# Sparse attention followed by a three-way max layer: bf16 value copies on VectorE and another order of the units

## The chip, the cores and the metric

The kernel runs on one core of a Trainium2 chip. The time is the device time of one execution in microseconds (us); of several executions the median is given. A profile of one execution comes beside it: its span is the time from the first to the last instruction of the program.

## What is computed

Attention over 4 batches, 8 heads, 768 positions of 64 numbers each. A position sees the first 8 positions of its batch (global) and the last 96 up to itself (local); each head subtracts its own slope times the distance. The rows of the result, 3072 of 512 numbers, go through a layer that takes the largest of three products and then multiplies by an output matrix.

```python
scores = scale * np.matmul(q, k.transpose(0, 1, 3, 2))
keep = is_global | is_local
scores = np.where(keep, scores + bias, -1000000000.0)
a = softmax(scores)
x = np.matmul(a, v).transpose(0, 2, 1, 3).reshape(3072, 512)
h = np.maximum(np.maximum(x @ w1, x @ w2), x @ w3)    # 512 -> 768
out = h @ w_out                                       # 768 -> 512
```

## The kernel before, in words

The 3072 rows are cut into 24 tiles T of 128 rows, six to a batch. Attention for a tile needs its own keys and those of the tile in front of it, with four global rows copied over four old ones. Two tiles share one load n (n = T/2). The feed-forward layer works on seven chunks of 4, 2, 2, 4, 4, 4 and 4 tiles, so its matmuls have 512 or 256 moving columns.

The whole program is a list of about 500 small units, the string `SCHEDULE` (lines 25 to 60). A loop at line 538 calls them in the order of the list. Every engine takes its own instructions strictly in that order, so the list sets all queues at once: TensorE (PE), VectorE (DVE), ScalarE (ACT), GpSimd (POOL) and SyncE (SP), which issues nearly all DMAs. The last number of a unit mostly names its engine: 0 is ScalarE, 1 is VectorE, 2 is GpSimd. The letters:

- `l`, `v`, `w`, `o` load queries and keys, values, the three weight matrices and the output matrix (SP, lines 155 to 174 and 477 to 488). `c`, `C`, `W`, `Q` cast what they brought to bf16 (lines 178 to 190, 490 to 495).
- `x` transposes queries or keys of one load (line 242): with a last number of 6, 7 or 8 by sixteen matmuls on half the rows and two copies, one per half of the rows (6: ScalarE and VectorE; 7: both ScalarE; 8: both VectorE); with 2 or 3 by eight full matmuls and one copy on ScalarE or VectorE; with 9 by a DMA transpose on SP.
- `S` computes the scores of four heads of a tile and their exponentials (ScalarE, line 316). With a last number of 1 the distances are added on TensorE from `bias` (made by `B`, line 318); otherwise `M` (line 328) multiplies by `wmask` (made by `K`, line 323) on VectorE.
- `Y` copies rows of values into the layout that even tiles need (line 198), `G` and `V` put the global keys and values in place (lines 228 and 234), `Z` copies the first keys of a batch (line 206).
- `A` multiplies by the values (line 359) and divides by the sum (VectorE, lines 371 and 372). `T` transposes the result into `xT` (line 375): with 0 or 1 on TensorE and one copy, with 6 to 8 in half rows, with 4 by a DMA transpose on SP (line 380).
- `F` is one of 126 blocks of the first layer (line 416): four matmuls into a buffer `psH`, of which there are three; the first of three products is copied by ScalarE (428), the other two are folded in by VectorE (430, 432). `O` is one tile of the output (450) and its store on SP; `E` is the last chunk's outputs (455).
- `D` with a count makes so many matmuls of 512 columns on constants (line 501), whose result nobody reads.

`F3.1.2` is then chunk 3, block 1 of 6, product 2; `S16.1.0` is tile 16, group 1, without the bias; `T22.4` is the DMA transpose of tile 22.

The copies of the values (`Y`, `V`) go through `same` (line 192): on VectorE and GpSimd two bf16 numbers are moved as one int32 word, on ScalarE as bf16.

Of the kernel before, what the change touches and what calls it, by code (L numbers as in the profile page):

```python
# [22 lines left out]


SCHEDULE = """
    K4 B3.1 K3 c0.0.2 B0.1 B4.1 K6 B6.2 K1 K0 K7 B1.0 B2.1 K2 B7.0 D7.3 D3.3 D0.8 c0.1.1 K5 x0.1.8
    B5.0 l1.1 c1.1.0 D8.2 x0.0.6 D4.2 S1.0.1 l1.0 c1.0.1 M1.0 Z0.1 S1.1.1 M1.1 x1.1.3 v0 C0.0.1 G1.0
    C0.1.1 x1.0.6 S0.0.1 M0.0 S2.1.1 v1 C1.0.1 Y0.1.2 Y0.0.2 Y1.0.1 V2.2 S2.0.1 G2.0 C1.1.2 A1.2
    Y1.1.2 l2.1 S0.1.1 S3.0.1 M3.0 c2.1.2 V3.2 M2.0 M0.1 A0.2 S3.1.1 G3.0 M3.1 M2.1 A2.0 l2.0 x2.1.7
    c2.0.2 w0.0 T0.1 W0.0.2 w0.1 A3.1 T2.0 x2.0.6 T1.0 T3.1 S4.1.0 Y2.0.1 S4.0.0 G4.1 F0.1.0 F0.0.0  # L30
    S5.1.0 W0.1.1 w0.2 S5.0.0 M4.1 F0.0.1 w1.0 W2.0.0 W1.0.0 M5.1 v2 F0.1.1 W0.2.2 C2.1.0 F0.0.2
    C2.0.0 F0.1.2 M5.0 Y2.1.1 F0.5.0 M4.0 V5.0 w1.1 F0.4.0 F0.3.0 V4.1 W1.1.1 F0.2.0 W2.1.0 A5.1
    A4.0 F0.3.1 F0.2.1 w1.2 W2.2.1 l3.1 F0.5.1 W1.2.0 T5.0 F0.4.1 c3.1.0 T4.0 F0.5.2 x3.1.2 l3.0
    c3.0.1 F0.3.2 l4.1 c4.1.1 F1.2.0 F1.2.1 Z1.0 x3.0.7 l4.0 c4.0.1 F0.4.2 F1.4.0 S7.1.0 x4.0.6
    S7.0.0 F1.4.1 F1.2.2 v3 C3.1.1 F1.1.0 l5.0 c5.0.1 G7.1 F1.1.1 S6.1.0 M6.1 Y3.1.1 x4.1.7 S6.0.0
    F0.2.2 F1.0.0 M7.0 x5.0.7 S8.1.0 M7.1 S8.0.0 G8.0 F1.1.2 F1.4.2 C3.0.2 F1.0.1 F1.5.0 Y3.0.1 o2
    l5.1 c5.1.1 A7.1 F1.3.0 F1.3.1 o0 Q0.1 F1.5.1 o1 Q1.1 Q2.0 M6.0 x5.1.7 S9.1.0 v4 S9.0.0 G9.0
    C4.1.0 M8.1 F1.0.2 T7.1 C4.0.0 F1.3.2 l6.1 v5 l7.0 l6.0 l7.1 l8.0 O0.2.0 A6.1 Y4.0.1 V8.1 O0.3.0
    c6.1.1 x6.1.9 M9.0 M8.0 O0.0.0 T6.6 v6 S10.1.0 S10.0.0 G10.1 Y5.0.1 Y4.1.1 F1.5.2 M10.1 V9.1
    O0.1.0 c7.0.1 M10.0 A8.1 T8.4 F2.1.0 F2.5.0 C5.0.1 x7.0.9 F2.4.0 F2.0.0 c6.0.0 F2.0.1 F2.4.1  # L40
    F2.5.1 M9.1 S11.1.0 c7.1.0 S11.0.0 x6.0.6 F2.1.1 F2.5.2 C5.1.1 A9.1 T9.4 F2.3.0 Y5.1.1 M11.0
    M11.1 O1.0.0 F2.3.1 F2.3.2 S13.0.0 S13.1.0 C6.0.0 x7.1.6 V10.1 v7 v9 F2.0.2 V11.1 Z2.0 F2.1.2
    F2.2.0 G13.1 A10.0 A11.1 O1.1.1 T10.6 S12.0.0 S12.1.0 M13.0 F2.4.2 F2.2.1 C6.1.1 c8.0.1 v8 l9.0
    Y7.0.1 T11.7 l8.1 l9.1 S14.0.0 S14.1.0 F2.2.2 F3.0.0 F3.4.0 M12.0 F3.2.0 C7.0.0 G14.0 Y6.1.0
    M13.1 A13.0 M14.0 C7.1.0 V14.1 F3.4.1 M14.1 F3.0.1 F3.0.2 T13.4 S15.1.0 S15.0.0 O2.0.0 l10.1
    Y7.1.1 V15.1 F3.1.0 C8.0.0 M15.0 M15.1 F3.2.1 C8.1.0 Y8.1.0 A14.0 A15.1 T15.4 Y6.0.1 M12.1
    O2.1.1 C9.1.0 F3.2.2 c8.1.1 F3.5.0 F3.3.0 A12.0 Y9.1.1 F3.3.1 F3.3.2 c9.1.0 c9.0.0 F3.4.2 F3.1.1
    F3.5.1 C9.0.0 F3.5.2 F3.1.2 T14.4 T12.4 F4.0.0 x9.1.9 Z3.1 G15.1 F4.4.0 F4.4.1 x9.0.9 F4.4.2
    S19.1.0 S19.0.0 F4.0.1 M19.1 Y10.0.1 M19.0 F4.2.0 F4.2.1 S18.0.0 S18.1.0 F4.0.2 x8.1.9 x8.0.9
    S16.0.0 M18.1 S16.1.0 G16.1 F4.1.0 l10.0 V17.1 c10.0.1 c10.1.1 Y9.0.0 M16.0 l11.0 F4.5.0 F4.3.0  # L50
    l11.1 c11.1.1 v10 x10.0.9 x10.1.9 A19.1 O3.1.0 v11 F4.5.1 x11.1.9 T19.4 c11.0.1 x11.0.9 M18.0
    S17.1.0 S17.0.0 M17.1 O3.2.0 M17.0 V20.1 Y8.0.0 F4.3.1 F4.3.2 V16.0 G19.0 A18.1 T18.4 F4.1.1
    A17.0 C10.0.0 O3.3.0 M16.1 C11.1.1 F4.2.2 C10.1.0 S20.0.0 T17.4 S20.1.0 G20.0 Y10.1.1 F4.1.2
    F4.5.2 A16.2 Y11.0.0 M20.1 C11.0.0 S21.1.0 S21.0.0 G21.1 T16.4 O3.0.0 V22.1 M21.0 O4.1.0 M21.1
    M20.0 O4.0.1 Y11.1.1 S22.1.0 S22.0.0 G22.1 F5.5.0 V21.1 F5.0.0 O4.2.0 F5.0.1 M22.1 V23.0 O4.3.0
    A20.2 T20.4 M22.0 S23.0.0 M23.0 S23.1.0 M23.1 F5.3.0 F5.4.0 A21.0 T21.4 F5.0.2 F5.3.1 F5.3.2
    F5.2.0 F5.2.1 A22.1 A23.0 T23.4 T22.4 F5.2.2 F5.5.1 F5.1.0 F5.1.1 F5.1.2 F5.5.2 F5.4.1 F5.4.2
    F6.0.0 F6.4.0 O5.2.0 F6.1.0 F6.3.0 F6.3.1 F6.1.1 F6.3.2 F6.5.0 O5.1.0 F6.5.1 F6.5.2 F6.0.1
    F6.0.2 F6.2.0 F6.2.1 F6.4.1 F6.4.2 O5.3.1 F6.1.2 F6.2.2 O5.0.0 E D9.1
"""  # L60


# [1 line left out]
def kernel(  # L64
# [13 lines left out]
    nc = tc.nc  # L78
# [63 lines left out]
    def words(ap):  # L142
        return ap.bitcast(mybir.dt.int32)
# [32 lines left out]
    copies = (nc.scalar.copy, nc.vector.tensor_copy, nc.gpsimd.tensor_copy)  # L176
# [13 lines left out]
        copies[how](heads(vo(n)[:, e * H * 65:(e + 1) * H * 65])[:, :, 0:D], rawv[n][:, :, e * D:(e + 1) * D])  # L190

    def same(how, dst, src):
        if how:
            copies[how](words(dst), words(src))  # L194
        else:
            nc.scalar.copy(dst, src)

    def u_Y(n, half, how):
        b, k = divmod(n, 3)
        rows = slice(64 * half, 64 * half + 64)  # L200
        if k == 0:
            same(how, vf[b % 2][rows], vo(n)[0:64, half * H * 65:(half + 1) * H * 65])
        else:
            same(how, ve[k - 1][rows], vo(n - 1 + half)[64 - 64 * half:128 - 64 * half])
# [29 lines left out]
    def put_vg(T, how):  # L234
        n, hi = divmod(T, 2)
        dst = (vo(n) if hi else ve[n % 3 - 1])[0:NG // 2]
        same(how, dst, vo(n - n % 3)[0:NG // 2])
# [335 lines left out]
```

## Time and profile before

| | us |
|---|---|
| median of 3 runs | 175.34 (175.29 to 175.38) |
| the profiled execution, its own time | 175.3 |
| span of that execution | 173.5 |
| TensorE busy in the span | 168.0 |
| VectorE busy | 130.2 |
| ScalarE busy | 119.6 |
| GpSimd busy | 12.4 |

The profiled execution's time is 1.8 us above its span, and within 0.04 us of the median. The profile counts an engine as busy while an instruction of its own runs; matmuls overlap, so the distance between the starts of two matmuls tells what one costs, not its duration. In a line of a timeline the first number is the start, the second the length of the merged stretch, and brackets hold the idle time before it and who ended it. L423 is line 423 of the kernel.

### The profile page before, as it was taken

To read this page: it belongs to the slowest core of one execution; us is meant where nothing else is said; L and a number is where in the kernel's file an instruction comes from. 1 tells how busy PE (TensorE), PEld (TensorE's weight loads), DVE (VectorE), ACT (ScalarE), POOL (GpSimd) and SP (SyncE) were. 2 spreads that over 40 slices of the span, in tenths; PEclk is the share of its full clock that TensorE was granted. 3 is DMA by queue.
4 is the path that set the end of the run, shared out by engine and by line. 5 is a ranking of instruction groups with operands and counts; after the bars stand their busy time and mean duration, and the time that the engine had idled before them with its cause. 6 is when DMAs were issued, how large, how long until landed. Compare 5 with 4: busy or idle time off the path is not lost.

```text
span 173.5 us, 4167 instructions
## 1 busy us (share of the span) xinstructions
PE 168.0 (97%) x1636; PEld 93.0 (54%) x1659; DVE 130.2 (75%) x285; ACT 119.6 (69%) x192; POOL 12.4 (7%) x23
## 2 busy tenths in 40 slices
PE   8999999999999999999999999999999999999992
PEld 3345744567775777654544445455455544444442
DVE  6477859998999999979998496997759773346600
ACT  6998999889998898797780576978975112321042
POOL 5417520001000000000000000000000000000000
PEclk9999999999999999999999999999999999999999
DMA  4999999999999996979969899995423120110126
GB/s 122 343 299 339 360 349 384 387 343 389 313 289 292 255 247 167 285 198 293 204 163 170 202 292 186 214 198 132 160 92 95 32 60 0 60 60 0 64 80 222
DMA packets 56595, 36.18 MB, mean 209 GB/s; under 512 B 19456, under 2 KB 49024, under 8 KB 56576
## 3 DMA queue, kind: packets, MB, share of 16 engines
q1 hardware_dynamic: 55392, 35.33, 77.1%
q10 hardware_dynamic: 1184, 0.59, 1.3%
q8 instruction: 13, 0.21, 0.5%
q14 instruction: 6, 0.05, 0.1%
HBM read 25.17 MB, written 6.29 MB: 181 GB/s over the span
## 4 chain that ended last, share of the span: by engine, by line
PE 77%; DVE 12%; ACT 7%; issue 2%; POOL 0%; POOLq 0%; ACTq 0%; DVEq 0%
PE h L423 50%; PE po L438 14%; PE sp L305 5%; PE op L359 4%; ACT P L316 3%; DVE P L333 3%; ACT wmask L325 2%; DVE h L430 1%; DVE ve L194 1%; DVE xb L372 1%; PE tpr L260 1%; DVE qkp L187 1%; PE xtp L410 1%; DVE ht L432 1%; ACT bias L321 1%
## 5 line engine op out<-in xcount | busy, mean ns | idle before, releaser
L423 PE MATMUL h<-xT,w 128*128 128x512 bf16 (+1 forms) x491 | 99.6, 348 | 0.9 <-DVE h L430 0.2
L423 PEld LDWEIGHTS <-w 128*128 128x128 bf16 x504 | 47.1, 98 | 42.1 <-issue 0.4
L316 ACT ACTIVATE P<-sp 128x1024 bf16<-128x1024 f32 (+1 forms) x48 | 44.1, 964 | 6.2 <-PE sp L305 5.9
L428 ACT CAST h<-h 128x512 bf16<-128x512 f32 (+1 forms) x42 | 21.6, 537 | 26.5 <-PE h L423 26.0
L430 DVE TENSOR_TENSOR h<-h,h 128x512 bf16<-128x512 bf16 (+1 forms) x42 | 25.2, 606 | 19.5 <-PE h L423 16.8
L438 PE MATMUL po<-wo,ht 128*128 128x512 bf16 (+2 forms) x147 | 33.1, 362 | 0.5
L432 DVE TENSOR_TENSOR ht<-h,h 128x512 bf16<-128x512 bf16 (+1 forms) x42 | 25.3, 607 | 3.1 <-PE h L423 2.0
L333 DVE TENSOR_TENSOR P<-P,wmask 128x1024 bf16<-128x1024 bf16 x34 | 22.6, 682 | 1.6 <-ACT P L316 1.5
L438 PEld LDWEIGHTS <-ht 128*128 128x128 bf16 x156 | 14.3, 98 | 14.4
L447 ACT COPY ost<-po 128x512 f32<-128x512 f32 (+2 forms) x21 | 11.7, 566 | 13.9 <-PE po L438 13.4
L359 PEld LDWEIGHTS <-P 128*128 128x128 bf16 x352 | 12.9, 97 | 3.8 <-ACT P L316 0.4
L372 DVE TENSOR_TENSOR xb<-op,rz 128x512 bf16<-128x512 f32 x20 | 13.8, 691 | 0.7
L305 PE MATMUL sp<-qkT 64*128 64x128 bf16 x320 | 13.1, 217 | 0.0
L305 PEld LDWEIGHTS <-qkT 64*128 64x128 bf16 x320 | 9.2, 94 | 6.4 <-issue 4.0
L187 DVE CAST qkp<-rawp 128x1024 bf16<-128x1024 f32 x15 | 10.2, 681 | 2.1 <-DMA rawp<-in_k_dram 1.3
L503 PE MATMUL wp<-const-bfloat16-1.0 128*128 128x512 bf16 x18 | 7.5, 574 | 0.8 <-PEq L554 0.8
L447 DVE COPY ost<-po 128x512 f32<-128x512 f32 (+1 forms) x5 | 3.0, 607 | 6.1 <-PE po L438 6.1
L267 ACT COPY qkT<-tpr 128x512 bf16<-128x512 bf16 x12 | 6.8, 616 | 0.0
L190 ACT CAST vo<-rawv 128x512 bf16<-128x512 f32 x11 | 6.6, 638 | 0.0
L187 ACT CAST qkp<-rawp 128x1024 bf16<-128x1024 f32 x6 | 6.2, 1042 | 0.0
L371 DVE RECIPROCAL rz<-op 128x8 f32<-128x8 f32 x20 | 4.0, 198 | 1.7 <-PE op L359 1.7
L359 PE MATMUL op<-vo,P 128*128 128x65 bf16 x128 | 5.2, 193 | 0.0
(86 smaller groups left out, 118.9 us busy)
## 6 DMA issues: line engine op xcount, KB each, us to landing
rawv<-in_v_dram SPq DMA_DIRECT2D x12, 512.0 KB, 7.0
out_dram<-ost SPq DMA_DIRECT2D x23, 256.0 KB, 2.5
rawp<-in_k_dram SPq DMA_DIRECT2D x8, 512.0 KB, 7.6
rawp<-in_q_dram SPq DMA_DIRECT2D x12, 256.0 KB, 6.4
wst<-in_moe_w_dram SPq DMA_DIRECT2D x3, 1024.0 KB, 11.5
rawp<-in_q_dram SPq DMA_DIRECT2D x6, 512.0 KB, 6.8
wst<-in_moe_w_dram SPq DMA_DIRECT2D x3, 512.0 KB, 8.4
rawp<-in_k_dram SPq DMA_DIRECT2D x6, 256.0 KB, 8.6
```

The costliest lines, as they stand in the source:

```text
L187: copies[how](qk, src)
L305: nc.tensor.matmul(sp[:, z, i, ds], k_cols(T, hsl, jp, ds), q_cols(T, hsl, jp), start=not how, stop=True, skip_group_check=True)
L316: nc.scalar.activation(dst, src, AF.Exp, bias=0.0, scale=scale)
L333: nc.vector.tensor_mul(P, P, wmask[:, g, :, 0:2])
L359: nc.tensor.matmul(o, P[:, i, ds], vs[ds][:, h], start=(ds == 0), stop=(ds == len(vs) - 1), skip_group_check=True)
L372: nc.vector.tensor_tensor(out=x.rearrange("p (g h) d -> p g h d", g=2), in0=o4[:, :, :, 0:64], in1=rz[:, :, :, None].to_broadcast([128, 2, ...
L423: nc.tensor.matmul(ps, w123[f // 2][:, dm, j, (f % 2) * 128:(f % 2) * 128 + 128], xT[c][:, dm], start=(dm == order[0]), stop=(dm == order[ ...
L428: nc.scalar.copy(h01, ps)
L430: nc.vector.tensor_max(h01s[c, f], h01s[c, f], ps)
L432: nc.vector.tensor_max(ht[c][:, f], h01s[c, f], ps)
L438: nc.tensor.matmul(po, ht[c][:, f, tt * 128:(tt + 1) * 128], wo[:, f, cols], start=(f == 0), stop=(f == NF - 1))
L447: copy(ost, po)
```

## The change

`same` now moves values on VectorE as bf16, twice as many elements of half the size; GpSimd still moves int32 words, ScalarE bf16. The list of units is put into another order, and 71 units get another engine or form. No unit is added or dropped, save that the idle matmuls of `D` are split otherwise.

```diff
     def same(how, dst, src):
-        if how:
-            copies[how](words(dst), words(src))
-        else:
-            nc.scalar.copy(dst, src)
+        if how == 2:
+            nc.gpsimd.tensor_copy(words(dst), words(src))
+        else:
+            copies[how](dst, src)
```

The beginning of the list, before and after (up to the first `F`):

```diff
-    K4 B3.1 K3 c0.0.2 B0.1 B4.1 K6 B6.2 K1 K0 K7 B1.0 B2.1 K2 B7.0 D7.3 D3.3 D0.8 c0.1.1 K5 x0.1.8
-    B5.0 l1.1 c1.1.0 D8.2 x0.0.6 D4.2 S1.0.1 l1.0 c1.0.1 M1.0 Z0.1 S1.1.1 M1.1 x1.1.3 v0 C0.0.1 G1.0
-    C0.1.1 x1.0.6 S0.0.1 M0.0 S2.1.1 v1 C1.0.1 Y0.1.2 Y0.0.2 Y1.0.1 V2.2 S2.0.1 G2.0 C1.1.2 A1.2
-    Y1.1.2 l2.1 S0.1.1 S3.0.1 M3.0 c2.1.2 V3.2 M2.0 M0.1 A0.2 S3.1.1 G3.0 M3.1 M2.1 A2.0 l2.0 x2.1.7
-    c2.0.2 w0.0 T0.1 W0.0.2 w0.1 A3.1 T2.0 x2.0.6 T1.0 T3.1 S4.1.0 Y2.0.1 S4.0.0 G4.1 F0.1.0 F0.0.0
+    l1.1 D0.8 B0.0 K4 K5 B5.2 K2 B7.1 D6.4 D7.1 D1.2 K0 B2.1 c0.1.1 K6 c0.0.1 K3 K1 B4.1 B6.0 B1.1
+    K7 B3.1 x0.1.2 x0.0.6 D8.2 S1.0.1 M1.0 S1.1.1 l1.0 M1.1 c1.0.1 G1.0 c1.1.2 Z0.1 x1.1.3 x1.0.6
+    S0.0.1 S2.1.1 S2.0.1 v0 C0.1.2 Y0.1.1 G2.0 C0.0.1 Y0.0.1 Y1.0.1 M0.0 A1.2 D5.1 S0.1.1 S3.0.1
+    M0.1 A0.2 v1 S3.1.1 C1.1.2 M2.0 M3.1 M2.1 C1.0.2 Y1.1.2 V2.2 A2.0 l2.1 c2.1.2 x2.1.7 V3.2 l2.0
+    c2.0.2 w0.0 W0.0.2 G3.0 T0.1 M3.0 A3.1 w0.1 w0.2 W0.1.2 T1.0 x2.0.7 T2.1 T3.1 S4.0.0 M4.0
+    S4.1.0 G4.0 F0.0.0 Y2.0.1 F0.1.0 F0.0.1 F0.1.1 V4.0 w1.0 W1.0.1 F0.0.2 M4.1 v2 C2.0.1 F0.1.2
```

Of the rest, these places are spoken of below (new list, TensorE's and SP's units and what feeds them):

```diff
+    x3.1.2 F0.4.2 Z1.0 l4.0 c4.0.0 x3.0.6 F0.5.2 T4.4 F1.4.0 l4.1 F1.2.0 S7.1.0 c4.1.1 S7.0.0 x4.0.6
...
+    Y8.0.0 F3.4.2 O2.0.0 O2.1.0 M15.1 M15.0 A12.1 G15.1 V16.1 C8.0.0 T12.4 M14.0 c9.0.1 F3.2.0
+    F3.0.0 c8.1.0 V14.1 F3.5.2 x8.1.9 F3.3.0 A15.1 F3.3.1 T15.4 A14.0 F3.0.1 F3.0.2 c9.1.0 C9.0.0
+    T14.4 x9.0.9 F3.2.1 F3.1.2 F3.2.2 c8.0.0 C9.1.0 C8.1.0 F4.4.0 F4.5.0 F4.4.1 F3.3.2 x9.1.9
+    S19.1.0 S19.0.0 M19.1 F4.2.0 F4.5.1 x8.0.9 S16.1.0 S16.0.0 G16.1 l10.1 v11 v10 M16.0 Z3.1 l10.0
...
+    M23.0 O4.2.0 F5.5.1 F5.5.2 A23.0 F5.4.0 V22.1 F5.0.1 A22.1 T23.4 F5.2.2 F5.0.2 F5.3.2 F5.4.1
+    F5.4.2 T22.4 F6.0.0 F6.0.1 F6.5.0 F6.5.1 F6.4.0 F6.3.0 F6.0.2 F6.1.0 F6.1.1 O5.3.0 O5.2.0 F6.3.1
...
+    F6.3.2 F6.4.1 F6.5.2 F6.1.2 F6.4.2 F6.2.0 O5.0.0 F6.2.1 F6.2.2 O5.1.1 E D2.6
```

The old list had `T4.0` in the place of `T4.4`, and ended in `F6.1.2 F6.2.2 O5.0.0 E D9.1`.

More of the change, by code (lines that the diff above doesn't have):

```diff
@@ L31 @@
[L31 to L59, printed above, removed]
+    l1.1 D0.8 B0.0 K4 K5 B5.2 K2 B7.1 D6.4 D7.1 D1.2 K0 B2.1 c0.1.1 K6 c0.0.1 K3 K1 B4.1 B6.0 B1.1
@@ new lines @@
+    K7 B3.1 x0.1.2 x0.0.6 D8.2 S1.0.1 M1.0 S1.1.1 l1.0 M1.1 c1.0.1 G1.0 c1.1.2 Z0.1 x1.1.3 x1.0.6
+    S0.0.1 S2.1.1 S2.0.1 v0 C0.1.2 Y0.1.1 G2.0 C0.0.1 Y0.0.1 Y1.0.1 M0.0 A1.2 D5.1 S0.1.1 S3.0.1
+    M0.1 A0.2 v1 S3.1.1 C1.1.2 M2.0 M3.1 M2.1 C1.0.2 Y1.1.2 V2.2 A2.0 l2.1 c2.1.2 x2.1.7 V3.2 l2.0
+    c2.0.2 w0.0 W0.0.2 G3.0 T0.1 M3.0 A3.1 w0.1 w0.2 W0.1.2 T1.0 x2.0.7 T2.1 W0.2.2 T3.1 S4.0.0 M4.0
+    S4.1.0 G4.0 F0.0.0 Y2.0.1 F0.1.0 F0.0.1 F0.1.1 V4.0 w1.0 W1.0.1 F0.0.2 M4.1 v2 C2.0.1 F0.1.2
+    W2.0.0 S5.1.0 M5.1 S5.0.0 M5.0 F0.4.0 C2.1.0 Y2.1.1 V5.1 F0.5.0 w1.1 F0.3.0 W2.1.1 F0.2.0 A4.1
@@ new lines @@
+    A5.0 F0.5.1 W1.1.0 w1.2 W1.2.0 F0.4.1 W2.2.1 F0.3.1 F0.2.1 F0.3.2 l3.1 c3.1.0 T5.0 l3.0 c3.0.1
+    x3.1.2 F0.4.2 Z1.0 l4.0 c4.0.0 x3.0.6 F0.5.2 T4.4 F1.4.0 l4.1 F1.2.0 S7.1.0 c4.1.1 S7.0.0 x4.0.6
+    F1.2.1 F1.4.1 F1.2.2 G7.0 F1.0.0 M7.1 F1.1.0 l5.0 c5.0.1 S6.1.0 x4.1.6 S6.0.0 v3 C3.0.2 M7.0
+    F1.0.1 F0.2.2 x5.0.7 C3.1.1 S8.1.0 S8.0.0 G8.0 F1.1.1 F1.1.2 o0 l5.1 o2 Y3.0.1 F1.4.2 c5.1.1
+    F1.0.2 F1.5.0 A7.1 Q2.0 o1 v4 v5 F1.3.0 F1.5.1 x5.1.7 Q0.1 Q1.1 S9.0.0 Y3.1.0 C4.0.0 S9.1.0
+    F1.5.2 M6.0 M6.1 F1.3.1 F1.3.2 G9.1 l6.1 T7.0 l7.0 l6.0 l7.1 O0.1.0 M8.0 C4.1.0 A6.0 M9.0 M9.1
@@ new lines @@
+    O0.0.0 Y4.1.1 c6.1.1 S10.0.0 T6.8 S10.1.0 x6.1.9 O0.2.0 M8.1 M10.0 v6 V9.1 O0.3.0 F2.4.0 F2.3.0
+    Y4.0.0 M10.1 F2.4.1 C5.0.1 G10.0 F2.4.2 V8.1 c6.0.0 A9.1 T9.4 F2.0.0 F2.0.1 c7.0.1 F2.5.0
+    S11.0.0 x6.0.6 S11.1.0 F2.3.1 Y5.0.1 V10.1 F2.0.2 F2.1.0 A8.0 M11.1 T8.4 C5.1.0 Y5.1.1 c7.1.0
+    O1.1.0 V11.1 M11.0 x7.0.9 v7 l8.0 F2.2.0 F2.1.1 S13.1.0 S13.0.0 x7.1.6 Z2.0 G13.1 F2.1.2 F2.2.1
+    A10.1 A11.2 C6.1.1 O1.0.0 S12.0.0 T10.8 v8 S12.1.0 F2.5.1 C6.0.1 F2.5.2 F2.3.2 l8.1 l9.1 l9.0
+    T11.6 v9 S14.0.0 S14.1.0 M13.1 M13.0 F2.2.2 Y6.1.1 M12.1 C7.0.1 F3.5.0 Y6.0.1 C7.1.0 F3.4.0
@@ new lines @@
+    A13.0 T13.4 F3.1.0 G14.1 F3.5.1 M14.1 S15.1.0 Y7.1.1 V15.0 S15.0.0 F3.4.1 M12.0 Y7.0.0 F3.1.1
+    Y8.0.0 F3.4.2 O2.0.0 O2.1.0 M15.1 M15.0 A12.1 G15.1 V16.1 C8.0.0 T12.4 M14.0 c9.0.1 F3.2.0
+    F3.0.0 c8.1.0 V14.1 F3.5.2 x8.1.9 F3.3.0 A15.1 F3.3.1 T15.4 A14.0 F3.0.1 F3.0.2 c9.1.0 C9.0.0
+    T14.4 x9.0.9 F3.2.1 F3.1.2 F3.2.2 c8.0.0 C9.1.0 C8.1.0 F4.4.0 F4.5.0 F4.4.1 F3.3.2 x9.1.9
+    S19.1.0 S19.0.0 M19.1 F4.2.0 F4.5.1 x8.0.9 S16.1.0 S16.0.0 G16.1 l10.1 v11 v10 M16.0 Z3.1 l10.0
+    F4.1.0 Y8.1.0 M19.0 O3.3.1 F4.1.1 c10.1.1 l11.1 S18.1.0 M18.1 S18.0.0 F4.1.2 l11.0 F4.4.2 Y9.0.1
@@ new lines @@
+    Y9.1.0 C10.1.0 A19.1 T19.4 F4.3.0 F4.3.1 O3.0.0 x10.1.9 M18.0 G19.0 M16.1 S17.1.0 c10.0.0
+    x10.0.9 S17.0.0 M17.1 F4.2.1 F4.2.2 M17.0 C10.0.1 F4.0.0 F4.0.1 A18.1 T18.4 V17.0 Y10.1.1 F4.5.2
+    c11.1.0 Y10.0.0 F4.3.2 O3.1.0 A17.1 C11.0.1 V20.1 x11.1.9 C11.1.0 O3.2.0 c11.0.1 x11.0.9 T17.4
+    F4.0.2 S20.0.0 S20.1.0 G20.1 A16.2 Y11.1.1 Y11.0.0 T16.4 O4.0.1 S21.0.0 M21.0 S21.1.0 G21.1
+    O4.3.1 O4.1.0 M20.1 M21.1 M20.0 S22.0.0 M22.0 S22.1.0 F5.1.0 F5.0.0 V21.1 M22.1 G22.1 F5.5.0
+    F5.2.0 A20.0 V23.0 F5.1.1 F5.1.2 A21.0 F5.2.1 T21.4 F5.3.0 F5.3.1 T20.4 S23.1.0 M23.1 S23.0.0
```

## The prediction

> **What bounds the kernel now.** First the page's head and the engines by stretch, then the chain that ended last, then single rows of the timelines.
>
> ```profile
> span 173.5 us, 4167 instructions
> ...
> PE 168.0 (97%) x1636; PEld 93.0 (54%) x1659; DVE 130.2 (75%) x285; ACT 119.6 (69%) x192; POOL 12.4 (7%) x23
> ...
> PE 77%; DVE 12%; ACT 7%; issue 2%; POOL 0%; POOLq 0%; ACTq 0%; DVEq 0%
> ```
>
> The engines by stretch (start:end, length, then busy us of each):
>
> ```profile
> 8.00:20.85 12.85, 12.50 (x229) 7.55 (x223) 9.72 (x26) 12.23 (x22) 7.15 (x10) 1.00 1.13 332
> 20.85:47.00 26.15, 25.89 (x282) 15.65 (x288) 22.53 (x45) 24.39 (x39) 1.71 (x2) 1.00 1.08 364
> 47.00:67.00 20.00, 19.84 (x282) 14.34 (x284) 19.70 (x47) 17.89 (x32) 0.00 (x0) 1.00 1.21 264
> 67.00:98.00 31.00, 30.50 (x287) 16.84 (x290) 26.89 (x59) 21.14 (x35) 0.00 (x0) 1.00 0.91 207
> ```
>
> Columns after the length: PE, weight loads, VectorE, ScalarE, GpSimd, granted clock, DMA. TensorE leads in every stretch, but busy is not proof, since matmuls overlap. The chain of waits in order of time has the proof:
>
> ```profile
> 20.85 0.38 PE h L423
> ...
> 88.16 6.26 PE h L423 x29
> ```
>
> 29 matmuls of 512 columns in 6.26 us are 0.216 us each, without a hole. From the first block of the first layer at 20.85 to the end of the matmuls near 170.1, TensorE's timeline names an idle wait on another engine in one place only:
>
> ```profile
> 34.78 0.39 PE L410 MATMUL xtp<-identb,xb 128*128 128x128 bf16 x4
> 35.01 1.03 PE L423 MATMUL h<-xT,w 128*128 128x512 bf16 x4
> ...
> 67.25 1.56 PE L423 MATMUL h<-xT,w 128*128 128x256 bf16 x12 [0.24 <-DVE h L430]
> ```
>
> So the kernel is three pieces: an opening of 20.85 us before the first `F`, some 149 us of saturated TensorE, and the stores behind it. A new order can shorten the opening, take matmuls off TensorE, fill that one hole, or open new holes. It can't gain much: what TensorE has to do stays.
>
> **The change, part by part.**
>
> *The copies.* These groups are copies inside SBUF:
>
> ```profile
> L194 DVE COPY ve<-vo 64x520 int32<-64x520 int32 x8 | 3.4, 425 | 0.4 <-ACT vo L190 0.2
> ...
> L194 DVE COPY vf<-vof 64x260 int32<-64x260 int32 x4 | 1.1, 285 | 0.1
> ...
> L207 DVE COPY kf<-qkT 128x512 bf16<-128x512 bf16 x2 | 0.6, 285 | 0.0
> ```
>
> VectorE copied 512 bf16 in 285 ns and 260 words (520 bf16) in 285 ns: per byte the same. 1040 bf16 should thus take the 425 ns of 520 words, and I put the edit of `same` at zero. The other end, if time went by elements: from 260 to 520 words are 140 ns, so 1040 elements come to 425 + 280 = 705 ns, 0.28 us more for each copy. I keep that end for a rival; the nearest row in type and place, the one of `kf`, speaks for zero. Below zero there is no reason.
>
> *The opening.* ScalarE is busy 12.23 of 12.85 us there and sets the pace.
>
> ```profile
> 7.94 0.51 ACT L321 ACTIVATE bias<-rbq 128x384 bf16<-128x384 f32 x1
> 8.36 1.03 ACT L187 CAST qkp<-rawp 128x1024 bf16<-128x1024 f32 x1
> 9.29 0.57 ACT L267 COPY qkT<-tpr 128x512 bf16<-128x512 bf16 x1
> 9.77 1.92 ACT L316 ACTIVATE P<-sp 128x1024 bf16<-128x1024 f32 x2
> ...
> 20.05 0.60 ACT L411 COPY xT<-xtp 128x512 bf16<-128x512 bf16 x1
> ```
>
> Ahead of the first exponential at 9.77 the new order takes away one bias (8.36 - 7.94 = 0.42) and the cast of `c1.1` (9.29 - 8.36 = 0.93, now on GpSimd, where it replaces `c0.0`), and adds the one copy of `x0.1.2` (1024 elements, an estimate of 0.93 from that cast). Net 0.42 earlier, at 9.35. But the transposes of `x0.1` stand behind the idle matmuls, 15 where there were 14:
>
> ```profile
> 0.77 6.12 PE L503 MATMUL wp<-const-bfloat16-1.0 128*128 128x512 bf16 x14 [0.77 <-PEq L554]
> ...
> 20.22 0.62 PE L305 MATMUL sp<-qkT 64*128 64x128 bf16 x16
> 20.85 1.89 PE L423 MATMUL h<-xT,w 128*128 128x512 bf16 x7
> ```
>
> At 6.12 / 14 = 0.44 us each they end near 7.25, the eight transposes near 8.0, and ScalarE's copy starts then and not at 7.9; the first exponential comes at about 9.5, 0.25 earlier. The cast of `c0.0`, now on VectorE behind `c0.1` (the three `B` left for VectorE follow it), is done by 7.2, so it isn't late. Later `D5.1` (one matmul, 0.22) stands before `S0.1`, and the scores of tiles 3 wait for buffers, so I keep 0.1 to 0.2 of it. The last step is new: both copies of `x2.0.7` are now on ScalarE, and the first `F` needs the buffer of the second. Sum: first `F` at about 20.7, **-0.15**. Bounds: it can't be before its weights are cast,
>
> ```profile
> 19.39 1.04 POOL L492 CAST w<-wst 128x1024 bf16<-128x1024 f32 x1 [0.38 <-DMA wst<-in_moe_w_dram]
> ```
>
> 20.43, since that cast waits for a load that keeps its place in the queue: -0.4. If ScalarE's extra copy costs its full 0.48 (9.77 - 9.29) at the end: +0.3.
>
> *TensorE's work after the opening.* The same `F`, `O` and `A`, and the scores of tiles 5 to 23, in as many alternations (20) between half-row and full matmuls. `T4.0` becomes `T4.4`: four matmuls less, from 34.78 to 35.01, **-0.23**. In its place SP issues a DMA transpose behind `l4.0`; the data is needed about 6.5 us after `A4`, and it waits behind loads already queued. I cost it at nothing. That cover is the blocks of chunk 0 in between; without it TensorE would stand until the landing.
>
> *The hole at 67.25.* VectorE is busy 19.70 of 20.00 us in the stretch before, so it is late there with a buffer. The new list gives VectorE after the first `F` two `Y`, one `V` and several casts less, ScalarE more. Walking the new queues by the rows above up to chunk 2, I find every buffer free 0.1 us or more before it is due, but with little to spare. I count half of the hole: **-0.12** (bounds -0.24 and +0.6, two more such waits each a full 512-column VectorE step of 0.69 late with half of it hidden).
>
> *The end.* `E` is unchanged, and one `O` still covers the last `F`. `D2.6` puts six matmuls where one was:
>
> ```profile
> 170.10 0.38 PE L503 MATMUL wp<-const-bfloat16-1.0 128*128 128x512 bf16 x1
> ```
>
> ```profile
> 170.64 0.37 ACTq L448 DMA_DIRECT2D out_dram<-ost  x1
> ```
>
> 6 x 0.216 = 1.3 us from 170.1 is 171.4, while the last store, issued at 170.64, lands 2.0 us later:
>
> ```profile
> out_dram<-ost ACTq DMA_DIRECT2D x1, 64.0 KB, 2.0
> ```
>
> Hidden by 1.2 us; bound +0.1.
>
> Sum: -0.15 - 0.23 - 0.12 = -0.50. The profiled execution's own time is 175.3, the median of the runs 175.34, so **174.8** it is.
>
> **The rivals.**
>
> *A. Late DMA transposes (slower).* Three are nearer to their use than any before: `T4.4`, `T14.4` before `F4.4.0`, and `T22.4` before `F6.0.0`. Between the start of `A22.1` and `F6.0.0` now stand the tile itself (0.48) and five blocks, 5 x 0.864, so 4.80 us; before it was eight blocks and two tiles. What has to fit in:
>
> ```profile
> 136.57 0.69 DVE L430 TENSOR_TENSOR h<-h,h 128x512 bf16<-128x512 bf16 x1 [1.11 <-PE h L423]
> 137.17 0.20 DVE L371 RECIPROCAL rz<-op 128x8 f32<-128x8 f32 x1
> 137.41 0.69 DVE L372 TENSOR_TENSOR xb<-op,rz 128x512 bf16<-128x512 f32 x1
> ```
>
> ```profile
> 136.30 0.65 PE L359 MATMUL op<-ve,P 128*128 128x65 bf16 x16
> ```
>
> ```profile
> DMA to landing us min/median/max: 2.4/2.4/7.5
> ```
>
> From the tile's start to the end of `xb` are 137.41 + 0.69 - 136.30 = 1.80 us, and the transpose lands 2.4 later: 4.2 to 4.3, half a microsecond to spare. The same sum holds for `A14.0` and `T14.4`, which also follows `x8.1.9` and `T15.4` on SP. It decides as soon as VectorE or SP is more than 0.5 us behind at one of them; with the 7.5 us of the slowest landing it would cost 3 us. A usual price is 1 us at one of the two and 0.5 at the other: 174.8 + 1.5 = 176.3.
>
> *B. Nothing is left.* The opening ends where it did (the weights' load and the third `psH` buffer rule it) and the hole only moves: 175.3 - 0.23 + 0.1 to 0.3 = 175.2 to 175.4. For it: every term of the sum is at most 0.23 and rests on queues with little slack. Against it: `T4` leaves TensorE for certain.
>
> *C. The bf16 copies take 705 ns.* In VectorE's full stretch from 47 to 67 the new list has seven of them (`Y4.1`, `V9`, `V8`, `Y5.0`, `V10`, `Y5.1`, `V11`): 7 x 0.28 = 2.0 us straight onto TensorE's buffers, 174.8 + 2.0 = 176.8. The Trainium skill says in "VectorE: DVE Perf Modes", under the errata of TRN2, that bf16 data read as INT32 halves the elements and the VectorE time; by that sentence undoing it doubles the copies' time, as here. The same page's perf-mode tier table gives a bf16 copy in SBUF 4x and an fp32 one 2x, by which both forms take the same; the rows of 285 ns agree with the table, not with the sentence.
>
> **How the numbers follow.** Forecast 174.8 (own range 174.4 to 174.98): 0.45, and 0.03 for an opening at its bound of -0.4 with the hole closed too, 174.4 or below. B: 0.27. A: 0.19. C: 0.06. A measurement of this kernel can tell about 0.2%, 0.35 us, from no change; "same" is 174.99 to 175.69, where B lies. Faster: 0.48; same: 0.27; slower (A and C): 0.25. The range leaves out C and the dearest part of A above and little below: 174.3 to 176.4.
>
> **What would show it.** The copies: groups of line 194 on VectorE at about 425 and 285 ns. The opening: the first row of line 423 near 20.7, the first exponential near 9.5. `T4`: 24 transposes on line 410 instead of 28. The hole: no bracket near 67 on TensorE's rows. Rival A: a bracket before line 423 near 94, 144 or 38, ended by a DMA. The forecast is wrong if TensorE's rows show brackets of over 0.3 us in sum after the first `F`, or if that comes after 20.9.

## The result and the profile after

| kernel | us, median (lowest to highest) | ratio to before, 95% interval |
|---|---|---|
| before, on the same chip | 175.38 (175.29 to 175.58), 7 runs | |
| the changed kernel | 174.84 (174.65 to 175.06), 7 runs | 0.9964 [0.9955, 0.9974] |
| the same kernel again, on another chip | 174.70 (174.61 to 175.43), 12 runs | 0.997 [0.9958, 0.9982] |

The change makes the kernel 0.36% faster, 0.54 us; 0.5 was forecast. The profiled execution of the changed kernel is its slowest, 175.06 us; where that matters, the profile of the second set (174.62 us) stands beside it. (The excerpt of the new list's beginning shown with the change leaves out one unit: `W0.2.2` stands between `T2.1` and `T3.1`.)

The page's head, and the shares of the chain that ended last:

```profile
span 173.2 us, 4168 instructions
...
PE 167.7 (97%) x1629; PEld 92.7 (54%) x1652; DVE 130.7 (75%) x284; ACT 122.3 (71%) x190; POOL 14.4 (8%) x24
...
PE 80%; ACT 10%; DVE 6%; issue 2%; POOL 0%; ACTq 0%; POOLq 0%
```

TensorE holds 80% of the chain (77% before), VectorE half of its former 12%, ScalarE 10% (7% before): some work went from VectorE's queue to ScalarE's. The same can be seen in the stretch ahead of the hole (start:end, length, then busy us of PE, weight loads, VectorE, ScalarE, GpSimd):

```profile
47.00:67.00 20.00, 19.84 (x282) 14.37 (x284) 19.35 (x47) 19.78 (x35) 0.00 (x0) 1.00 1.08 251
```

VectorE 19.70 to 19.35, ScalarE 17.89 to 19.78, TensorE the same. Now the three places of the sum. The opening, on TensorE's timeline:

```profile
0.77 5.13 PE L503 MATMUL wp<-const-bfloat16-1.0 128*128 128x512 bf16 x15 [0.77 <-PEq L554]
6.46 0.62 PE L281 MATMUL tpp<-identb,qkp 128*128 128x128 bf16 x8 [0.55 <-DVE qkp L187]
...
20.53 5.35 PE L423 MATMUL h<-xT,w 128*128 128x512 bf16 x23
```

and on ScalarE's:

```profile
7.46 0.59 ACT L325 ACTIVATE wmask<-rbq 128x384 bf16<-128x384 f32 x1
7.96 0.99 ACT L284 COPY qkT<-tpp 128x1024 bf16<-128x1024 bf16 x1
8.85 0.57 ACT L267 COPY qkT<-tpr 128x512 bf16<-128x512 bf16 x1
9.44 1.94 ACT L316 ACTIVATE P<-sp 128x1024 bf16<-128x1024 f32 x2
```

The first exponential starts at 9.44 instead of 9.77, the first block of the first layer at 20.53 instead of 20.85: 0.33 gained and 0.32 kept. `T4`, by the group of the full-row transposes, 24 matmuls of 219 ns where there were 28:

```profile
L410 PE MATMUL xtp<-identb,xb x24: 219/219/230, 17.7 to 50.9; 128*128 128x128 bf16 x24
```

The hole near 67, first on TensorE, then on VectorE:

```profile
66.58 0.61 PE L423 MATMUL h<-xT,w 128*128 128x256 bf16 x4
67.42 0.60 PE L423 MATMUL h<-xT,w 128*128 128x256 bf16 x4 [0.23 <-DVE h L430]
```

```profile
64.84 0.68 DVE L333 TENSOR_TENSOR P<-P,wmask 128x1024 bf16<-128x1024 bf16 x1
65.56 0.42 DVE L196 COPY ve<-vo 64x1040 bf16<-64x1040 bf16 x1
66.02 0.42 DVE L196 COPY vo<-vof 4x1040 bf16<-4x1040 bf16 x1
66.36 0.67 DVE L333 TENSOR_TENSOR P<-P,wmask 128x1024 bf16<-128x1024 bf16 x1
66.97 0.40 DVE L430 TENSOR_TENSOR h<-h,h 128x256 bf16<-128x256 bf16 x1
```

Four matmuls of 256 columns, 0.108 each (half of 0.216), from 66.58 end their turn at 67.01, and the next start at 67.42: 0.4 us in which TensorE waits for the fold of `F2.1.1`, line 430. That fold runs at 66.97, last in a row of `M11.1`, `Y5.1`, `V11` and `M11.0`. The hole is still there. From start to start it was 0.31 us before and is 0.39 now. The first profile has another one at 45.4: four matmuls from 44.80 end their turn at 45.23, and the next start at 45.40, 0.17 us later. The second set's profile, of the same kernel, doesn't have it, and most of the 0.18 us between the last output matmuls of the two profiles arises there.

The account, by the profile of the second set: the last output matmul starts at 169.51 instead of 170.04, 0.53 earlier. Of that 0.33 come from the opening and 0.22 from `T4` (four matmuls less; this is a count, no run measures it alone); the hole at 67 gives nothing.

### The profile page after: what moved, and what is told of

It reads as the page before. It is cut to its first block, busy times and chain, and to the rows that moved or that the text cites. A ratio compares the mean times of both kernels' runs of the same rounds, so it can differ in the third digit from the quotient of the medians.

```text
span 173.2 us, 4168 instructions
## 1 busy us (share of the span) xinstructions
PE 167.7 (97%) x1629; PEld 92.7 (54%) x1652; DVE 130.7 (75%) x284; ACT 122.3 (71%) x190; POOL 14.4 (8%) x24
## 4 chain that ended last, share of the span: by engine, by line
PE 80%; ACT 10%; DVE 6%; issue 2%; POOL 0%; ACTq 0%; POOLq 0%
PE h L423 51%; PE po L438 14%; PE sp L305 6%; PE op L359 4%; ACT wmask L325 2%; ACT P L316 2%; PE sp L298 2%; DVE xb L372 1%; ACT ost L447 1%; PE tpr L260 1%; PE oph L359 1%; PE wp L503 1%; DVE ve L196 1%; DVE P L333 1%; DVE h L430 1%
## 5 line engine op out<-in xcount | busy, mean ns | idle before, releaser
L333 DVE TENSOR_TENSOR P<-P,wmask 128x1024 bf16<-128x1024 bf16 x34 | 23.2, 701 | 6.6 <-ACT P L316 6.6
L187 DVE CAST qkp<-rawp 128x1024 bf16<-128x1024 f32 x12 | 8.2, 686 | 2.6 <-DMA rawp<-in_k_dram 1.4
L187 ACT CAST qkp<-rawp 128x1024 bf16<-128x1024 f32 x9 | 9.4, 1050 | 0.4 <-DMA rawp<-in_k_dram 0.4
L267 ACT COPY qkT<-tpr 128x512 bf16<-128x512 bf16 x11 | 6.3, 600 | 0.4 <-PE tpr L260 0.3
L190 ACT CAST vo<-rawv 128x512 bf16<-128x512 f32 x9 | 5.7, 634 | 0.1
L503 PEld LDWEIGHTS <-const-bfloat16-1.0 128*128 128x128 bf16 x24 | 2.6, 115 | 4.1 <-issue 3.0
```

What stands on the lines that cost most here:

```text
L187: copies[how](qk, src)
L333: nc.vector.tensor_mul(P, P, wmask[:, g, :, 0:2])
```

## The experiments

Each kernel starts from the changed one unless said otherwise; "first `F`" and "last `E`" are the starts of the first matmul of the first layer and the last of the output in its profile. Line numbers of some are one lower than in the changed kernel.

| kernel | us, median | ratio, 95% interval | first `F` | last `E` |
|---|---|---|---|---|
| before | | | 20.85 | 170.04 |
| changed | 174.84 | 0.9964 [0.9955, 0.9974] | 20.53 | 169.69 |
| changed, again | 174.70 | 0.997 [0.9958, 0.9982] | 20.52 | 169.51 |
| int32 copies | 174.68 | 0.9959 [0.9947, 0.9971] | 20.53 | 169.54 |
| bf16 copies in the old list | 175.39 | 1.0003 [0.9992, 1.0013] | 20.85 | 170.05 |
| old opening | 175.21 | 0.9996 [0.9983, 1.001] | (21.92) | (171.16) |
| old rest | 175.50 | 1.0004 [0.9996, 1.0012] | 20.52 | 170.21 |
| `T4` on TensorE | 177.15 | 1.0127 [1.0093, 1.0162] | 20.54 | 171.99 |
| `A22` later | 176.24 | 1.0041 [1.0027, 1.0056] | 20.52 | 170.98 |
| two `M` further back | 174.61 | 0.9955 [0.9944, 0.9967] | 20.53 | 169.44 |
| two copies on GpSimd | 174.59 | 0.9964 [0.9945, 0.9983] | 20.53 | 169.54 |
| both of these | 174.48 | 0.9951 [0.994, 0.9963] | 20.53 | 169.31 |
| first casts as before | 178.84 | 1.0191 [1.0177, 1.0205] | 24.22 | 173.55 |
| `W0.2` on ScalarE | 178.44 | 1.0171 [1.0132, 1.0209] | 20.53 | 172.49 |

The profiled run of the old opening is 1.1 us above its own median, so its two numbers stand in brackets; only their difference is used.

### The form of the copies

New order, old `same`:

```diff
-        if how == 2:
-            nc.gpsimd.tensor_copy(words(dst), words(src))
+        if how:
+            copies[how](words(dst), words(src))
```

> The new order with the old copies (two bf16 as one int32 word on VectorE). If the gain is the order's alone, the time stays that of the changed kernel within 0.15 us (174.84) and the copies on VectorE keep 0.42 us for 520 words, as the profile after shows 0.42 for 1040 bf16. If the bf16 form itself gives something, for instance beside GpSimd's casts, where one copy took 1.21 us, the time moves by 0.3 us or more either way.

And the reverse, the old list with the new `same`:

> The old order with the new copies (bf16 on VectorE). If the form of the copies costs and gives nothing, the time stays at 175.37 within 0.15 us. If 1040 bf16 take 705 ns as elements would have it, the stretch from 47 to 67 us gets some 2 us longer and the time is near 177.

The first takes 174.68 us, the second 175.39: order alone has the whole gain, form alone none. The groups of line 196 (min/median/max ns), in the old list with bf16 copies:

```profile
L196 DVE COPY ve<-vo x8: 424/425/427, 20.7 to 124.6; 64x1040 bf16<-64x1040 bf16 x8
L196 DVE COPY vf<-vof x4: 278/286/291, 44.0 to 89.2; 64x520 bf16<-64x520 bf16 x4
```

425 and 286 ns, where the int32 words of before took 425 and 285. In the changed kernel:

```profile
L196 DVE COPY ve<-vo x8: 424/424/1207, 22.5 to 120.4; 64x1040 bf16<-64x1040 bf16 x8
```

The one copy of 1207 ns isn't the form: with int32 words in the new order it takes 1.20 us too. It is taken up below.

### The opening and the rest, each alone

The old list up to the first `F` with the new one behind it; then the new list up to there with the old one behind:

> The old list up to the first F, the new list behind it (units that the new opening held besides are put just ahead of that F). If the opening gives its 0.32 us whatever follows, the first F comes at 20.85 instead of 20.53 and the time is about 175.15. If TensorE's later waits swallow an earlier start, or if the loads set the pace behind it, the time stays near 174.85.

> The new list up to the first F, the old list behind it (units that the old opening held besides are put just ahead of that F). If the opening carries the gain and the rest gives nothing in sum, the first F comes at 20.55 to 20.7 and the time is 174.95 to 175.1. If the rest gives its own share, as TensorE's four matmuls of T4 would have it, the time is above 175.15. If the two parts only work together, it is at 175.35 or above.

Neither half moves the time by more than can be told: 0.9996 and 1.0004, both intervals across 1. By the medians the new rest alone is 0.16 us below the old kernel beside it (175.21 for 175.37, near the 175.15 of the expectation), and the new opening alone is 0.16 above (175.50 for 175.34). Together they give 0.5 to 0.6 us. For the new opening the trace shows why it loses its gain. Its first `F` is as early as in the changed kernel, and then, TensorE's timeline first and ScalarE's second:

```profile
20.52 1.90 PE L422 MATMUL h<-xT,w 128*128 128x512 bf16 x8
22.56 0.62 PE L304 MATMUL sp<-qkT 64*128 64x128 bf16 x16
...
115.63 0.62 PE L304 MATMUL sp<-qkT 64*128 64x128 bf16 x16 [0.19 <-PE h L422]
```

```profile
20.46 1.94 ACT L315 ACTIVATE P<-sp 128x1024 bf16<-128x1024 f32 x2
22.29 0.22 ACT L231 COPY qkT<-qkT 128x32 bf16<-128x32 bf16 x1
```

Eight matmuls from 20.52 are through at 22.25 (8 x 0.216); the scores of tile 5 start at 22.56. ScalarE's exponentials of tile 4 hold the score buffers until 22.40, and the copy of the global keys behind them (`G4`, until 22.51) is what the profile names as the end of the wait. Before, the same eight matmuls were through at 22.58 and the scores started at 22.67. So TensorE was 0.33 us ahead of the old kernel and is now 0.11 ahead: 0.22 are lost on the spot. At 115.63 another 0.27 are lost (the old kernel has that row at 115.46); what ends that wait the profile doesn't settle. The new list has six blocks of `F` behind the opening, 24 matmuls (23 of them recorded) in one row from 20.53 to 25.82 in the changed kernel, and the wait is gone. An opening that ends earlier is worth something only if what follows it doesn't wait for the engine that set the opening's pace.

Behind the old opening the new rest takes 149.24 us from the first `F` to the last `E` in its profile, and 149.19 are those of before; the changed kernel takes 149.16 in the first profile and 148.99 in the second set's. That run has the first profile's hole at 45.4 too, 1.4 us later. That is one execution, and one well above its median, so how much of `T4`'s 0.22 the other executions keep is not shown; their median leaves room for most of it.

### `T4` back on TensorE, in its new place

```diff
-    x3.0.6 F0.5.2 T4.4 F1.4.0
+    x3.0.6 F0.5.2 T4.0 F1.4.0
```

> The changed kernel with T4.0 in the place of T4.4: the transpose of tile 4 back on TensorE and its copy on ScalarE. If TensorE is saturated there, four matmuls come back and the time rises by 0.22 to 0.25, to about 175.07. If the DMA transpose costs what it saves by pushing the loads behind it, the time stays or falls.

It costs 2.3 us and not 0.2. The four matmuls are the small part:

```profile
39.19 0.38 PE L409 MATMUL xtp<-identb,xb 128*128 128x128 bf16 x4 [1.05 <-ACT qkT L266]
40.24 1.03 PE L422 MATMUL h<-xT,w 128*128 128x256 bf16 x8 [0.68 <-ACT xT L410]
```

The transposes wait 1.05 us until ScalarE has emptied a buffer that `x3` filled, and the next block waits 0.68 for ScalarE's copy of the tile. So the DMA form did more than drop four matmuls: in this order it takes `T4` past two waits that the TensorE form would meet. (Four of the six executions took 177.05 to 177.24 us at a mean granted clock of 1.00, two took 178.6 at 0.99.)

### A later `A22`: the slack of rival A

`A22.1` two blocks, 8 x 0.216 = 1.73 us, further back:

> The changed kernel with A22.1 two blocks of the first layer later, so that three blocks instead of five stand between it and F6.0.0: 0.48 + 2.59 = 3.07 us for the 4.23 us that the trace shows from A22's start to the landing of T22. If the slack of 0.57 us was real and nothing else hides the wait, TensorE stands for 1.15 to 1.25 us before F6.0.0 and the time rises by that to about 176.0. If the transposes land earlier when asked earlier or TensorE finds other work, less.

```profile
141.72 2.32 PE L422 MATMUL h<-xT,w 128*128 128x512 bf16 x10
145.11 5.12 PE L422 MATMUL h<-xT,w 128*128 128x512 bf16 x23 [1.07 <-DMA xT<-xb]
```

Ten matmuls from 141.72 are through at 143.88; the next start at 145.11, 1.23 us later, when the transpose has landed. 1.73 of delay gave 1.23 of stall: the slack is half a microsecond, as the prediction worked out (4.80 against 4.2 to 4.3). (The time rises by somewhat more than the stall, 176.24 for 174.70: this profile has the hole at 45.4 as well. Its last `E` is 1.29 later than that of the first profile.) In the changed kernel the tile starts at 139.02, its data is due at 143.82 and landed at 143.25.

```profile
139.02 0.65 PE L359 MATMUL op<-ve,P 128*128 128x65 bf16 x16
```

### The hole at 67

Two multiplies by `wmask` moved behind folds that TensorE waits for:

```diff
-    M7.0 F1.0.1 F0.2.2 x5.0.7 C3.1.1
+    F1.0.1 F0.2.2 x5.0.7 C3.1.1 M7.0
...
-    M11.0 x7.0.9 v7 l8.0 F2.2.0 F2.1.1
+    x7.0.9 v7 l8.0 F2.2.0 F2.1.1 M11.0
```

> The changed kernel with two multiplications by the mask on VectorE put a few units later: M7.0 behind the cast C3.1.1, M11.0 behind the fold of F2.1.1. If the holes of TensorE at 45.4 (0.17 us) and 67.4 (0.39 us) come from VectorE's order alone, both go and the time falls by 0.4 to 0.55 us, to about 174.35. If VectorE is late there as a whole, the holes only move and the time stays within 0.15 us.

The fold now goes ahead of `M11.0`, at 66.34 instead of 66.97, and TensorE's row has no break:

```profile
66.34 0.40 DVE L429 TENSOR_TENSOR h<-h,h 128x256 bf16<-128x256 bf16 x1
66.67 0.67 DVE L332 TENSOR_TENSOR P<-P,wmask 128x1024 bf16<-128x1024 bf16 x1
```

```profile
66.55 1.05 PE L422 MATMUL h<-xT,w 128*128 128x256 bf16 x8
```

So the hole at 67 comes from `M11.0` ahead of the fold. But the expected 0.4 to 0.55 us don't come: the last `E` is only 0.07 us earlier than in the second set's profile (169.44 for 169.51), and the time, 174.61, can't be told from 174.70. Row by row beside that profile, TensorE gains the 0.39 of the hole, loses about 0.15 ahead of it (0.10 of it between 46.1 and 46.7) and 0.17 behind it, at 68.5 and 70.4, in waits of about 0.1 each. The other hole of the expectation, at 45.4, is gone as well, but it isn't in the second set's profile either, so `M7.0` isn't shown to be its cause.

The other way is to take copies out of VectorE's queue ahead of the fold:

```diff
-    C5.1.0 Y5.1.1 c7.1.0 O1.1.0 V11.1
+    C5.1.0 Y5.1.2 c7.1.0 O1.1.0 V11.2
```

> The changed kernel with two value copies ahead of the hole at 67 us (Y5.1 and V11) given to GpSimd. If the hole is VectorE's queue (theory), 0.7..0.8 us leave that queue, the hole of 0.4 us is gone and the time is 174.4..174.7 (the fold runs earlier, but part of a hole's worth has come back elsewhere before). If GpSimd's copies slow VectorE's work beside them (rival; one VectorE copy took 1.2 us instead of 0.42 beside a GpSimd cast at 22.4 us), VectorE's rows beside them are longer by 0.3 us or more each, a hole stays, and the time is 174.8..175.2.

GpSimd's rows, then VectorE's:

```profile
64.71 0.61 POOL L193 COPY ve<-vo 64x520 int32<-64x520 int32 x1 [21.96 <-ACT vo L189]
65.38 0.96 POOL L193 COPY vo<-vof 4x520 int32<-4x520 int32 x1
```

```profile
64.92 1.97 DVE L332 TENSOR_TENSOR P<-P,wmask 128x1024 bf16<-128x1024 bf16 x2
66.81 0.41 DVE L429 TENSOR_TENSOR h<-h,h 128x256 bf16<-128x256 bf16 x1
```

0.84 us left the queue, but the fold comes only 0.23 earlier beside TensorE's row (0.16 after the start of the matmuls ahead of it, 66.81 and 66.65, instead of 0.39, 66.97 and 66.58): the two multiplies that run beside GpSimd's copies take 1.97 us together, where they took 0.68 + 0.67. Both the theory and its rival are right in part; the time, 174.59, is that of the changed kernel within the interval. With both edits:

> The order of e4 (M7.0 and M11.0 further back) together with the two copies on GpSimd. If both holes and the small ones that took their place are VectorE's queue, none of them stays and the time is 174.2..174.5; if a hole's worth comes back in ScalarE's or TensorE's order, it is that of e4, 174.6.

TensorE's rows, with the copies moved and then with both edits:

```profile
66.65 1.22 PE L422 MATMUL h<-xT,w 128*128 128x256 bf16 x8
67.70 0.65 PE L358 MATMUL op<-ve,P 128*128 128x65 bf16 x16
```

```profile
66.55 1.05 PE L422 MATMUL h<-xT,w 128*128 128x256 bf16 x8
67.43 0.65 PE L358 MATMUL op<-ve,P 128*128 128x65 bf16 x16
```

The eight matmuls hold TensorE for 1.05 us (66.65 to 67.70) and for 0.88: the copies alone shrink the hole from 0.4 to 0.17 us, both edits close it. The time is then 174.48 us, with the earliest last `E`, 169.31. It has the best time of all, 0.9951 of before; against the moved multiplies alone (0.9955) and the changed kernel (0.9964) the intervals overlap.

### The casts

First the two casts of the opening on the engines that they had:

```diff
-    c0.0.1
+    c0.0.2
...
-    c1.1.2
+    c1.1.0
```

> The changed kernel with the two casts that it moved put back: c0.0 on GpSimd and c1.1 on ScalarE, the rest of the new order kept. If the engines of the first casts carry the gain of the opening (theory), ScalarE has some 0.9 us more in its queue ahead of the first exponentials, the first feed-forward matmul moves from 20.5 to 21.1..21.4 us, and the time from 174.8 to 175.3..175.5. If the order of the units alone carries it (rival), the first feed-forward matmul stays at 20.5 and the time at 174.7..174.85.

The direction is that of the theory, the size is not: 24.22 and 178.84 us. ScalarE's timeline, and TensorE's:

```profile
9.44 1.94 ACT L315 ACTIVATE P<-sp 128x1024 bf16<-128x1024 f32 x2
11.27 0.22 ACT L231 COPY qkT<-qkT 128x32 bf16<-128x32 bf16 x1
11.37 1.06 ACT L186 CAST qkp<-rawp 128x1024 bf16<-128x1024 f32 x1
14.08 0.59 ACT L266 COPY qkT<-tpr 128x512 bf16<-128x512 bf16 x1 [1.65 <-PE tpr L259]
```

```profile
12.48 1.02 PE L280 MATMUL tpp<-identb,qkp 128*128 128x128 bf16 x8 [2.22 <-ACT qkp L186]
```

In the new list `c1.1` stands behind the exponentials of tile 1. On ScalarE it has to wait for them, until 11.37, and TensorE, which transposes what it casts, stands for 2.22 us. Before, the same cast ran at 8.36, ahead of those exponentials. And the hole has a second price, in the granted clock (the number before the last two of each row):

```profile
11.00:13.44 2.44, 0.96 (x9) 0.77 (x10) 0.00 (x0) 1.43 (x3) 0.87 (x2) 0.82 1.21 290
13.44:16.00 2.56, 2.56 (x31) 1.03 (x32) 2.33 (x6) 1.18 (x2) 1.53 (x3) 0.51 1.11 345
```

It falls to 0.51 behind the hole; eight transposes take 1.02 us where they take 0.62 at full clock. In the changed kernel the clock is 1.00 in both stretches. The other cast, `c0.0`, costs nothing either way: the first exponential starts at 9.44 with it on GpSimd or on VectorE. So it is not the cast moved to VectorE that pays, it is that `c1.1` is off ScalarE in this order. The run doesn't price the 0.93 that the prediction took out of ScalarE's queue: in the old list this cast stood ahead of the exponentials, here it stands behind them.

Then the cast that ran beside the slow copy:

```diff
-    T2.1 W0.2.2 T3.1
+    T2.1 W0.2.0 T3.1
```

> The changed kernel with the one weight cast that runs on GpSimd at 22.4 us (W0.2) given to ScalarE. If that cast is what makes VectorE's copy beside it take 1.2 us (theory), the copy takes 0.42..0.45 us; the time changes by no more than 0.2 us, up if ScalarE is late by its 0.9 us for the scores behind it. If the copy is slow for a reason of its own (rival, such as a first use or the transposes beside it), it stays at 1.2 us.

The copy takes 0.43 us, as the theory has it. In the changed kernel, VectorE's rows and GpSimd's:

```profile
21.53 0.91 DVE L333 TENSOR_TENSOR P<-P,wmask 128x1024 bf16<-128x1024 bf16 x1 [1.08 <-ACT P L316]
22.47 1.21 DVE L196 COPY ve<-vo 64x1040 bf16<-64x1040 bf16 x1
```

```profile
22.36 1.04 POOL L492 CAST w<-wst 128x1024 bf16<-128x1024 f32 x1 [0.46 <-DMA wst<-in_moe_w_dram]
```

and VectorE's in the experiment:

```profile
24.34 0.69 DVE L332 TENSOR_TENSOR P<-P,wmask 128x1024 bf16<-128x1024 bf16 x1 [3.90 <-ACT P L315]
25.06 0.43 DVE L195 COPY ve<-vo 64x1040 bf16<-64x1040 bf16 x1
```

But my "no more than 0.2 us" was off by more than 3: the time is 178.44. I had counted the cast's 0.9 us and not the wait in front of it:

```profile
22.34 1.04 ACT L491 CAST w<-wst 128x1024 bf16<-128x1024 f32 x1 [1.93 <-DMA wst<-in_moe_w_dram]
```

```profile
25.87 2.75 PE L422 MATMUL h<-xT,w 128*128 128x512 bf16 x12 [2.58 <-ACT h L427]
```

The weights land at 22.3. GpSimd can stand and wait for them; on ScalarE the wait of 1.93 us stands in front of the exponentials of tile 4 and the first copies out of `psH`, and TensorE stands for 2.58. Three of its six executions, at a mean granted clock of 1.00, took 177.4 to 177.8 us, and three, at 0.99, 179.1 to 179.4. The profiled one is among the first three, so no trace shows where the clock fell in the others.

## Why the prediction was right, and where it wasn't

- **What bounds the kernel.** Right. TensorE's busy time is the same, and every gain or loss seen in the runs came through a TensorE row.
- **The copies at zero.** Right: 425 against 425 ns and 286 against 285, and each form in each order. Rival C is dead; the perf-mode tier table of the Trainium skill's "VectorE: DVE Perf Modes" agrees with these rows, its sentence on int32 words doesn't. (The 705 ns of rival C are 1.66 times 425, not the doubling that it names beside them.)
- **The opening, -0.15.** The mechanism was right, the size was not: -0.32. The failing steps are two. The walk let ScalarE's copy wait for the transposes behind idle matmuls of 0.44 us each, until 8.0. The 15 took 5.13 us, 0.34 each, TensorE then waited 0.55 for the cast, and the transposes were through at 7.08; the copy started at 7.96 because ScalarE's own row for `wmask`, from 7.46, stood ahead of it. So the 9.5 for the first exponential came out nearly right (9.44) by another way. And "I keep 0.1 to 0.2 of it" had no row behind it: all of it was kept. Neither `D5.1` nor the two copies of `x2.0` on ScalarE cost anything that shows; what each would cost alone was not measured.
- **`T4`, -0.23.** Right, as a count of matmuls: -0.22. That the TensorE form would have cost 2.3 us in the new place was not seen.
- **The hole, -0.12.** Wrong: nothing came back, 0.4 us are lost, by a bracket of the same size as before's (0.23, before 0.24). The step that failed is "I find every buffer free 0.1 us or more before it is due". The walk overlooked that `M11.0` stands ahead of `F2.1.1` on VectorE; moved back behind it, the hole is gone. Of the two signs named for it, a bracket near 67 shows it, and brackets of over 0.3 us in sum do not: the bracket says 0.23 where 0.39 are lost from start to start. (The profile records a matmul of 256 columns as 0.27 us long, while the starts of two lie 0.108 apart, so a bracket understates what is lost.)
- **The end, hidden.** Right. Six idle matmuls end at 171.2, the last store is issued at 170.24 and lands 1.8 later.

```profile
169.75 1.47 PE L503 MATMUL wp<-const-bfloat16-1.0 128*128 128x512 bf16 x6
```

- **The rivals.** A's arithmetic holds, with its slack of half a microsecond confirmed, and the chance it was given rested on delays that didn't come. B had one half: the hole stayed. Its other half, an opening that ends where it did, didn't come.

So the 0.5 was right as a sum of -0.15, -0.23 and -0.12, but is made of -0.33, -0.22 and about 0: two errors cancelled, and that is luck.

## What to carry to other kernels

When a unit moves to another engine, count the wait that it brings along as well as its own length: the cast of 1.04 us that waits 1.93 for a load cost 2.5 to 4.5 us in ScalarE's queue, and in GpSimd's TensorE waits for nothing. Read a change of order by what stands ahead of the one fold or copy that TensorE waits for, not by an engine's busy share: VectorE had 0.35 us less to do ahead of the hole, and the hole stayed. And an earlier start is kept only if the order behind it fits: the new opening and the new rest gave nothing that can be told alone, and 0.3 to 0.4% together.

## What the runs showed of the hardware

VectorE and GpSimd hinder each other. A VectorE copy of 0.42 us took 1.21 beside a GpSimd cast that had started 0.11 earlier, and ended 0.28 us after it; without that cast it took 0.43. Which of the two starts first decides who waits. In the opening of the changed kernel a VectorE copy at 13.28 took 0.83 us beside a GpSimd cast that had started at 13.22; in the run with two copies on GpSimd the same copy, again at 13.28, took 0.42, and the cast, which now started at 13.31, took 0.87 instead of 0.62. Multiplies of 0.68 took 0.95 and 1.10 us beside GpSimd copies, one of which took 0.96 instead of 0.61. The Trainium skill says in "SBUF — State Buffer", under "Who interferes with whom", that a VectorE copy in a two-port mode and a GpSimd instruction exclude each other for their whole length, and that a VectorE instruction with two inputs in SBUF contends with GpSimd's reads. The copies' rows agree; the multiplies were slowed by 0.27 and 0.42 us, less than the length of the copies beside them. Folds, which read one of their inputs from PSUM, took their usual 0.4 us: 0.42 at 65.93, in the run with both edits, beside a GpSimd copy that ran from 65.28 to 66.24.

A hole on TensorE can cost more than its length. Behind 2.2 us of it in the opening the granted clock was 0.51 from 13.44 to 16.00; the profile has half the clock from 12.54 to 15.96, 3.4 us, and full clock on both sides. An estimate from that: 3.4 us at half clock cost up to 1.7 us of a busy TensorE and lower the mean clock of an execution of 176 us to 0.99. That is what three of six executions show with `W0.2` on ScalarE (a hole of 2.6 us; about 1.7 us longer, at 0.99) and two of six with `T4` on TensorE (holes of 1.05 and 0.68 us; 1.5 us longer, at 0.99). That the holes did it there is likely, but no trace of such an execution was taken.
